# A Fourier mixing and maxout kernel on one core: the opening's loads, casts and table work put in another order

## The chip, the cores and the metric

The kernel runs on one NeuronCore of one Trainium2 chip. The metric is the time of one execution on the device in microseconds (us), median of several runs. The engines are TensorE (PE in the profile, its weight loads PEld), VectorE (DVE), ScalarE (ACT), GpSimd (POOL) and SyncE (SP), which here only issues DMAs. DMAs are issued by GpSimd (queue q0, which may also convert fp32 to bf16) and by SyncE (queue q1).

## The reference

Each of 8 batches of 3072 x 256 numbers is multiplied by a filter in the frequency domain, and the result goes through two matrices, a maximum and a third matrix:

```
X = np.fft.rfft(x, axis=1)
Y = X * (filt_r + 1j * filt_i)[None]
y = np.fft.irfft(Y, n=3072, axis=1)          # 8 x 3072 x 256
h1 = y @ w1;  h2 = y @ w2                    # 256 -> 1024
out = np.maximum(h1, h2) @ w_out             # 1024 -> 256
```

## The kernel before

The transform is split as 3072 = 96 x 32. The first stage multiplies by a 96-point table C1, the second (s2, L379) by a table U; a product with the filter F follows (product, L388), then the inverse stages with tables VP and VQ, and a last 96-point table G1 (s4, L454) that gives y for a tile of 384 rows. The second part uses max(h1, h2) @ w_out = relu(y (w1 - w2)) @ w_out + y (w2 @ w_out): Wd = w1 - w2 is made by GpSimd in four parts (prep_wd, L296), M = w2 @ w_out by TensorE (prep_t and prep_m, from the cast w2b and Wo). moe_h (L476) makes one of eight 128-wide parts of relu(y Wd) for a tile (ph, gt), moe_o (L519) the output sums (po).

All is written in a fixed order by hand (manual_schedule): each engine executes its instructions in program order, and waits only where data or a buffer needs it. PSUM tiles come from two pools: ps with six banks, pso with two.

Batch 0 has a path of its own. Its x comes in eight chunks of 4 x 256 columns on 96 partitions (load_x, L84; issued by GpSimd, converted to bf16); the filter F comes in sixteen DMAs (load_f, L111), also by GpSimd, into half of the partitions, and is doubled into the other half by VectorE for the first eight column groups (double_f, L128) and by SyncE's DMAs for the last four (L130). Rows with index 0 and 1536 come apart, in fp32 (FZ), and are put in by put_fz (L142, GpSimd) and fix_f (L145, VectorE). Then: s1t (L554) for the eight chunks, evicted by ScalarE (two of them by VectorE); transposes t1 (L566), evicted by VectorE and ScalarE in turn; s2 for six visits v; table_v and put_v, which make VP and VQ from U; products (L657), of which VectorE makes most and GpSimd those of v = 0, 2, 3, 4 for one half (from a copy xs that ScalarE makes) and a quarter of v = 5; s3t (L577) for v = 1, 0, 2, 3, 4, 5, each with a matmul on ones (W1) ahead that fills its wait, evicted into zT; transposes t2 (L599) and s4(0). U is made in two halves by ScalarE's sine (sines_u, L247). spin (L615) is a matmul whose result nobody reads.

x of batch 1 comes in four loads of two chunks (L680, L694, L698), and Wo by load_wo (L293), all by GpSimd between its products and prep_wd, then cast_w2. f1 (L323) is the first stage of batch 1: a matmul per pair of columns (pa), a copy to at, and after each second one a DMA to a DRAM tensor ad; f1_read (L340) reads it back in another order into bt, in three DMAs (u0 to u1).

From L777 on the main loop runs over 64 tiles and eight steps j each. At each step it emits moe_h, the listed visits (mid), part of moe_o of the tile before, and the planned small works (todo). Steps of batch 0 are numbered 0 to 63; plan(b, step, ...) puts a work at a step. plan_f2 (L733) places for the batch after next the loads of x to XF (load_xf, by SyncE, three buffers) and the folds (fold, GpSimd), and the visits of the batch that is next. ph is L482, po L534 and L536, and GpSimd issues the output DMAs (L495).

Of the kernel before, what the change touches and what calls it, by code (L numbers as in the profile page):

```python
# [8 lines left out]
FP32 = mybir.dt.float32  # L9
# [6 lines left out]
D = 256  # L16
HID = 1024
NP = 96
# [9 lines left out]
def kernel(  # L28
# [105 lines left out]
    def load_fn():  # L134
        for ri, f in enumerate((filt_r, filt_i)):
            for q in range(2):
                src = bass.AP(f.tensor, f.offset + 48 * q * D, [[96 * D, 16], [1, D]])
                nc.sync.dma_start(out=FZ[16 * q:16 * q + 16, ri], in_=src)
        nc.sync.dma_start(out=FZ[32:33, 0], in_=filt_r[1536:1537, :])
# [2 lines left out]
        G.tensor_copy(F[0:32, ri, 0, 0], FZ[0:32, ri])  # L142

    def fix_f():
        V.tensor_copy(F[32:33, 0, 0, 0], FZ[32:33, 0])  # L145


    V.memset(W1, 1.0)
# [5 lines left out]
    jb = init.tile([128, 16], FP32)  # L154
    cid = init.tile([128, 128], FP32)

    hv = init.tile([128, 2, 1], FP32)
    load_x(0, 0, 1)
    G.iota(pid, pattern=[[1, 1]], base=0, channel_multiplier=1, allow_small_or_imprecise_dtypes=True)
    G.iota(kc, pattern=[[2, NW], [24, 2], [1, 2]], base=0, channel_multiplier=0,  # L160
           allow_small_or_imprecise_dtypes=True)
    load_x(0, 1, 1)
    G.iota(kap, pattern=[[2, NW], [24, 2]], base=0, channel_multiplier=0,
           allow_small_or_imprecise_dtypes=True)
    G.iota(jb, pattern=[[1, 16]], base=0, channel_multiplier=0, allow_small_or_imprecise_dtypes=True)
    load_x(0, 2, 1)
    G.iota(cid, pattern=[[1, 128]], base=0, channel_multiplier=0, allow_small_or_imprecise_dtypes=True)
    for c in range(3, 8):
        load_x(0, c, 1)
    for q in range(2):  # L170
        G.memset(hv[:, q], 1.0)
        for r in (0, 32):
            G.memset(hv[r:r + 1, q], 0.5 * (1 - q))
    load_fn()
    for ri in range(2):
        put_fz(ri)
    load_f(0)
    load_f(1)

    def table_c():  # L180
        p96 = init.tile([128, 1], FP32)
        V.tensor_scalar(p96, pid, 1.0 / 96.0, None, OP.mult)
        uc = init.tile([NP, 48, 2], FP32)
        rc = init.tile([NP, 48, 2], FP32)
        kf = kc.rearrange("p w g s -> p (w g s)")
        V.tensor_scalar(uc[:, :, 0], kf, p96[0:NP], 0.25, OP.mult, OP.add)
        V.tensor_scalar(uc[:, :, 1], kf, p96[0:NP], None, OP.mult)
        V.tensor_scalar(uc[:, 0:1, 1], pid[0:NP], 0.5, 0.25, OP.mult, OP.add)
        V.tensor_scalar(rc, uc, RND, RND, OP.add, OP.subtract)
        V.tensor_tensor(uc, uc, rc, OP.subtract)  # L190
        S.activation(C1, uc.rearrange("p k r -> p (k r)"), AF.Sin, bias=zero[0:NP], scale=TWO_PI)

    def table_ct():
        G.memset(CT, 0.0)
# [52 lines left out]
    def sines_u(h):  # L247
        uv = ua.rearrange("p u c s j -> p u (c s j)")
        S.activation(U[:, NW * h:NW * h + NW], uv[:, NW * h:NW * h + NW], AF.Sin, bias=zero, scale=TWO_PI)

    def table_g():
        pg = ps.tile([96, NP], FP32, tag="ps", name="pg")
        TE.matmul(pg, C1, I128[0:NP, 0:NP], start=True, stop=True)
        S.activation(G1, pg, AF.Copy)

    def table_v(h, q):
# [16 lines left out]
    def put_v(h, q, pv):  # L273
        for s in range(2):
            i0 = 1 if h == 0 and s == 0 else 0
            tab = VQ if q else VP
            if i0:
                S.activation(tab[:, 0, 0], pv[0][:, 0], AF.Identity, bias=zero, scale=hv[:, q])
            S.activation(tab[:, 6 * h + i0:6 * h + 6, s], pv[s][:, i0:6], AF.Copy)  # L279
# [40 lines left out]
    zd = {}  # L320
    at_ = {}

    def f1(b, c, engine):  # L323
        if c == 0:
            ad[b] = dram.tile([96, NM, D], BF16, tag="ad", name="ad")
        if c % 4 == 0:
            at_[b] = apool.tile([128, 8, D], BF16, tag="at", name="at")
        at = at_[b]
        pa = ps.tile([96, 2, D], FP32, tag="ps", name="pa")
        TE.matmul(pa, C1, xb[b, c // 2][:, 2 * (c % 2):2 * (c % 2) + 2], start=True, stop=True)  # L330
        o_ = at[0:96, 2 * (c % 4):2 * (c % 4) + 2]
        if engine is V:
            V.tensor_copy(o_, pa)
        else:
            S.activation(o_, pa, AF.Copy)
        if c % 2 == 1:
            m0 = 2 * (c % 4) - 2
            nc.sync.dma_start(out=ad[b][:, 2 * c - 2:2 * c + 2], in_=at[0:96, m0:m0 + 4])

    def f1_read(b):  # L340
        bt[b] = bpool.tile([128, NU, D], BF16, tag="bt", name="bt")
        src = ad[b].rearrange("(u q) m d -> (q m) u d", q=4)
        for u0, u1 in ((0, 4), (4, 12), (12, NU)):
            nc.sync.dma_start(out=bt[b][:, u0:u1], in_=src[:, u0:u1])


    def s1(b, c):
# [227 lines left out]
            V.tensor_copy(bt[0][:, 4 * n:4 * n + 4], pb)  # L575

    def s3t(v, pq):  # L577
        pool, tag = (ps, "ps") if v % 2 else (pso, "po")
        pz = [pool.tile([128, 2, 2, 2, 2, NM], FP32, tag=tag, name="pt%d" % g) for g in range(2)]
        for _ in range(2 if v == 1 else 1):  # L580
            TE.matmul(pz[0].rearrange("p i s r c m -> p (i s r c m)"), W1[:, 0:128], W1, start=True, stop=True)  # L581
        for i in range(2):
            for s in range(2):
                for dc in range(2):
                    for q, tab in enumerate((VP, VQ)):
                        for g in range(2):
                            TE.matmul(pz[g][:, i, s, :, dc], pq[s][64 * g:64 * g + 64, q, i, 128 * dc:128 * dc + 128],  # L587
                                      tab[64 * g:64 * g + 64, 2 * v + i, s].rearrange("p (r m) -> p r m", r=2),
                                      start=(q == 0), stop=(q == 1))
        zv = zT.rearrange("p c m (w g) q -> p w g (c m) q", g=2)  # L590
        for g in range(2):
            o_ = zv[:, 2 * v:2 * v + 2, g]
            i_ = pz[g].rearrange("p i s r c m -> p i (c m) (s r)")
            if v >= 4 and g == 1:
                V.tensor_copy(o_, i_)
            else:
                S.activation(o_, i_, AF.Copy)

    def t2(c, engines):  # L599
        if c == 0:  # L600
            zr[0] = zrpool.tile([96, NM, D], BF16, tag="zr", name="zr")
        n = 4 // len(engines)
        for k, engine in enumerate(engines):
            pr = ps.tile([96, n, D], BF16, tag="ps", name="pr")
            m0 = 4 * c + n * k
            for m in range(n):
                for dc in range(2):
                    TE.transpose(pr[:, m, 128 * dc:128 * dc + 128], zT[:, dc, m0 + m].rearrange("p u q -> p (u q)"),  # L608
                                 I128)
            if engine is V:  # L610
                V.tensor_copy(zr[0][:, m0:m0 + n], pr)
            else:
                S.activation(zr[0][:, m0:m0 + n], pr, AF.Copy)
# [23 lines left out]
        if c < 7:  # L637
            spin(2)
    bt[0] = bpool.tile([128, NU, D], BF16, tag="bt", name="bt")
    zT = bpool.tile([128, 2, NM, NU, 4], BF16, tag="bt", name="zT")  # L640
    for n in range(6):
        t1(n, S if n % 2 else V)
    put_v(0, 0, table_v(0, 0))
    for g in range(2):
        for ri in range(2):
            double_f(0, g, ri, V)
# [22 lines left out]
    put_v(0, 1, table_v(0, 1))  # L669
    pxs[2] = s2(0, 2)  # L670
    stage_x(2)
    sines_u(1)
    put_v(1, 0, table_v(1, 0))
    pxs[3] = s2(0, 3)
    stage_x(3)
# [1 line left out]
    for v in (1, 0, 2):  # L677
        pqs[v] = products(v)
        if v == 0:
            load_x(1, 0, 2)  # L680
    s3t(1, pqs[1])
    pxs[4] = s2(0, 4)
    stage_x(4)
# [7 lines left out]
        pqs[v] = products(v)  # L691
    for v in (4, 5):
        s3t(v, pqs[v])
    load_x(1, 2, 2)  # L694
    load_wo()
    prep_wd(0, G)
    for c in (4, 6):
        load_x(1, c, 2)  # L698
    for q in range(1, 4):
        prep_wd(q, G)  # L700
    for h in range(2):
        cast_w2(h)
    table_ct()
# [4 lines left out]
    ypool = ctx.enter_context(tc.tile_pool(name="ypool", bufs=7))  # L708
    cepool = ctx.enter_context(tc.tile_pool(name="cepool", bufs=3))
    gpool = ctx.enter_context(tc.tile_pool(name="gpool", bufs=2))  # L710
    f1(1, 0, S)
    spin(1)
    t2(0, (V, S))
    f1(1, 1, V)
    spin(1)
    s4(0)
    f1(1, 2, S)
    f1(1, 3, V)


    todo = {}
# [4 lines left out]
    def plan_f1(b, nb, steps, read):  # L726
        for c, n in zip(range(4, 16), steps):
            plan(b, n, f1, nb, c, S if c % 2 == 0 else V)
        plan(b, read, f1_read, nb)

    mid = {}

# [15 lines left out]
            plan(b, steps[-1] + (6 if b else 11), s1_read, b + 2)  # L748

    plan(0, 1, t2, 1, (V,))  # L750
    plan(0, 7, prep_t, 0)
    plan(0, 9, prep_m)
    for c, n in ((2, 7), (4, 22), (5, 32), (6, 40), (7, 48)):
        plan(0, n, t2, c, (V,))
    plan_f1(0, 1, (5, 6, 7, 7, 9, 9, 10, 10, 11, 11, 12, 12), 13)
    plan_f2(0, (25, 28, 31, 35, 38, 42, 46), ((0,), (), (1,), (2,), (3,), (4,), (5, 6)),
            (8, 8, 10, 12, 17, 20, 24, 28), (10, 13, 16, 20, 24, 27, 30, 33))
    for b in range(1, B - 1):
        first = b == 1
        plan_f2(b, (15 if first else 14, 19 if first else 18, 23, 31, 34 if b < B - 2 else 35, 39, 47),  # L760
# [68 lines left out]
```

## Time and profile before

| | |
|---|---|
| median of the runs | 497.7 us (496.92 to 498.1, 3 runs) |
| the profiled execution's own time | 498.64 us |
| its span, first to last instruction | 496.8 us |
| TensorE busy | 483.8 us, 97% of the span, 5759 matmuls |
| VectorE, ScalarE, GpSimd busy | 335.4, 320.4, 258.7 us |
| mean granted clock of TensorE | 0.989 |
| first chunk of x taken by TensorE | 5.19 us |
| last chunk of x taken by TensorE | 14.21 us |
| first ph of the main loop | 37.73 us |
| first po | 44.19 us |

The profile is of one execution; the difference between its own time and its span lies around the first and the last instruction. A row of the timeline gives the start, the time until the last of its instructions ends, the engine, the line, the operation with its tiles, how many, and in brackets how long the engine had been idle and what ended that. Weight loads may run ahead of matmuls; matmul ends are modelled. "to landing" is the time from the start of a DMA's issue to the arrival of its data.

### The profile page before, as it was taken

The page shows a single profiled execution, that of the slowest core. Times are in us where ns is not written, and L with a number is a line of the kernel's source. Part 1 is how long each engine was busy: PE and PEld are TensorE (multiplying, and loading weights), DVE is VectorE, ACT ScalarE, POOL GpSimd, SP SyncE. Part 2 cuts the span into 40 slices and gives each one's busy share as a digit, 9 for nine tenths or more (in the row PEclk, how much of TensorE's full clock was granted, in tenths as well). Part 3 has the DMA queues.
Part 4 walks back from the last instruction along what each step waited for, and adds up shares of the span by engine and source line. Part 5 has one row for each costly group of instructions (what it writes and reads, how often), then busy time and mean ns, then how long its engine had stood idle before and what let it go on. Part 6 is the DMA issues. An engine that isn't in the chain of part 4 may idle for free.

```text
span 496.8 us, 14137 instructions
## 1 busy us (share of the span) xinstructions
PE 483.8 (97%) x5759; PEld 353.5 (71%) x5759; DVE 335.4 (68%) x535; ACT 320.4 (64%) x667; POOL 258.7 (52%) x342
## 2 busy tenths in 40 slices
PE   7699999999999999999999999999999999999997
PEld 3457777777777777777777777776777777777775
DVE  7886788468855688467855688457873688556542
ACT  5777478667775677576866668665766656464442
POOL 8694868318466594528646295536842212222220
PEclk9879999999999999999999999999999999999999
DMA  8989988996789867896789977897776834531112
GB/s 128 161 242 224 259 269 260 284 234 190 204 266 221 216 210 223 249 225 174 231 257 227 183 244 211 257 215 168 227 231 175 181 104 129 157 120 66 64 64 86
DMA packets 76626, 97.30 MB, mean 196 GB/s; under 512 B 7985, under 2 KB 54354, under 8 KB 75186
## 3 DMA queue, kind: packets, MB, share of 16 engines
q1 hardware_dynamic: 63218, 66.71, 52.1%
q0 software_dynamic: 13200, 29.60, 21.4%
q8 instruction: 45, 0.74, 0.7%
q14 instruction: 19, 0.16, 0.1%
q10 hardware_dynamic: 144, 0.09, 0.1%
HBM read 53.87 MB, written 47.19 MB: 203 GB/s over the span
## 4 chain that ended last, share of the span: by engine, by line
PE 92%; DMA 3%; ACT 2%; POOL 1%; issue 1%; DVE 0%; SPq 0%; POOLq 0%
PE po L536 34%; PE ph L482 33%; PE po L534 8%; PE pz L408 5%; PE pc L443 3%; PE px L384 2%; PE pa L355 2%; DMA xb<-in_x_dram 2%; DMA zr<-zd 1%; PE pt L587 1%; DMA zd<-zt 1%; PE pr L608 1%; POOL xb L89 1%; PE pt L581 1%; PE pa L330 1%
## 5 line engine op out<-in xcount | busy, mean ns | idle before, releaser
L486 ACT ACTIVATE gt<-ph 128x384 bf16<-128x384 f32 x357 | 175.7, 496 | 138.8 <-PE ph L482 136.2
L536 PE MATMUL po<-Wo,gt 128*128 128x256 bf16 x1528 | 262.7, 273 | 1.2 <-issue 1.2
L536 PEld LDWEIGHTS <-gt 128*128 128x128 bf16 x1528 | 144.7, 98 | 68.1 <-issue 13.5
L495 POOL DMA_DIRECT2D out_dram<-ot x186 | 103.1, 558 | 154.7 <-DVE ot L547 138.7
L390 DVE TENSOR_TENSOR pq<-px,F 128x1024 bf16<-128x1024 f32 x91 | 106.9, 1218 | 25.7 <-PE px L384 25.4
L484 DVE TENSOR_SCALAR gt<-ph 128x384 bf16<-128x384 f32 x155 | 83.6, 551 | 53.5 <-PE ph L482 47.1
L482 PEld LDWEIGHTS <-Wd 128*128 128x128 bf16 x1024 | 99.6, 98 | 13.7 <-issue 0.3
L104 POOL TENSOR_TENSOR xb<-XF 128x512 bf16<-128x512 f32 x48 | 61.3, 1277 | 66.9 <-DMA XF<-in_x_dram 31.7
L547 DVE TENSOR_SCALAR ot<-po 128x512 f32<-128x512 f32 x83 | 57.0, 686 | 35.0 <-PE po L536 33.1
L105 POOL TENSOR_TENSOR xb<-XF 128x512 bf16<-128x512 f32 x48 | 61.1, 1274 | 0.0
L359 ACT ACTIVATE at<-pa 128x512 bf16<-128x512 f32 x96 | 51.8, 611 | 3.4 <-PE pa L355 3.3
L412 ACT ACTIVATE zt<-pz 128x512 bf16<-128x512 f32 x84 | 45.6, 594 | 5.7 <-PE pz L408 1.9
L448 ACT ACTIVATE ce<-pc 128x384 f32<-128x384 f32 x56 | 23.7, 490 | 6.7 <-PE pc L443 6.0
L408 PE MATMUL pz<-pq,VP 64*64 64x256 bf16 x336 | 22.2, 281 | 0.0
L384 PE MATMUL px<-bt,U 64*64 64x256 bf16 x384 | 20.4, 283 | 1.2 <-ACT VQ L279 0.7
L408 PE MATMUL pz<-pq,VQ 64*64 64x256 bf16 x336 | 21.1, 269 | 0.0
L408 PEld LDWEIGHTS <-VP 64*64 64x64 bf16 x336 | 10.0, 105 | 13.3 <-issue 12.7
L355 PE MATMUL pa<-xb,CT 64*64 64x512 bf16 x192 | 18.0, 377 | 0.0
L443 PEld LDWEIGHTS <-zr 48*128 48x128 bf16 x896 | 13.1, 93 | 4.8 <-issue 4.4
L443 PE MATMUL pc<-G,zr 48*128 48x48 bf16 x896 | 15.4, 180 | 0.3 <-DMA zr<-zd 0.3
L384 PEld LDWEIGHTS <-U 64*64 64x64 bf16 x384 | 10.6, 109 | 3.9 <-issue 3.6
L618 PE MATMUL pd<-W 128*128 128x512 bf16 x28 | 9.2, 437 | 1.5 <-DVE zero L150 1.5
(383 smaller groups left out, 632.1 us busy)
## 6 DMA issues: line engine op xcount, KB each, us to landing
out_dram<-ot POOLq DMA_DIRECT2D x186, 128.0 KB, 3.8
XF<-in_x_dram SPq DMA_DIRECT2D x96, 192.0 KB
ad<-at SPq DMA_DIRECT2D x56, 192.0 KB
zd<-zt SPq DMA_DIRECT2D x42, 256.0 KB
zr<-zd SPq DMA_DIRECT2D x56, 192.0 KB
bt<-ad SPq DMA_DIRECT2D x13, 768.0 KB
WS<-in_moe_w_dram SPq DMA_DIRECT2D x4, 512.0 KB
xb<-in_x_dram POOLq DMA_DIRECT2D x8, 192.0 KB, 5.6
```

The lines of the kernel that those rows point to most:

```text
L104: G.tensor_tensor(t_[:, 0], f[:, 0], f[:, 1], OP.add)
L105: G.tensor_tensor(t_[:, 1], f[:, 0], f[:, 1], OP.subtract)
L359: S.activation(at[:, m0:m0 + 2], pa[g], AF.Copy)
L390: E.tensor_tensor(pq, px.rearrange("p (o i) d -> p o i d", o=1).to_broadcast([128, 2, 2, D]), F[:, :, 2 * v:2 * v + 2, s], OP.mult)
L408: TE.matmul(pz[g][64 * s:64 * s + 64, i], tab[64 * g:64 * g + 64, 2 * v + i, s], pq[s][64 * g:64 * g + 64, q, i], start=(q == 0), stop=(q ...
L412: S.activation(zt[:, :, g], pz[g], AF.Copy)
L482: TE.matmul(ph, Wd[:, dc, 128 * j:128 * j + 128], y_[:, dc], start=(dc == 0), stop=(dc == 1))
L484: V.tensor_scalar(gt[tt][:, j], ph, 0.0, None, OP.max)
L486: S.activation(gt[tt][:, j], ph, AF.Relu)
L495: E.dma_start(out=dst, in_=ot[tt // 2][:, 3 * (tt % 2) + c])
L536: TE.matmul(p_, g_[:, n - 2, blk], Wo[:, n - 2], start=(e == 0), stop=(e == 9))
L547: V.tensor_scalar(ot[tt // 2][:, e - 1:e + 1], po[q // 2 % 2], SCALE, None, OP.mult)
```

## The change

Ten edits, nearly all in front of the main loop:

- x of batch 0: pairs of chunks for the first six, single loads for the last two
- load_f(0) ahead of put_fz; fix_f by GpSimd
- the first load of x of batch 1 ahead of GpSimd's first product, the second in the place of the first; the later two change places with prep_wd and load_wo
- the second sine of U ahead of the transposes t1
- s3t takes its PSUM tiles from ps for v = 0, 3, 5 and from pso for 1, 2, 4 (before: ps for odd v)
- zT is laid out with eight groups of four columns outermost, and the last visit (v = 5) is evicted in two parts, group 0 first; a second 96-point table CP has its columns in the order that this layout needs, and G1 is made from it
- f1 is split in f1_in (matmul) and f1_out (copy and DMA); the first four copies come later
- the filling matmuls around t2(0) and s4(0) write one pso tile, four rather than two
- f1_read is planned as three works at steps 13, 14 and 15
- loads and folds of x of batch 2 at later steps

```diff
 def fix_f():
-        V.tensor_copy(F[32:33, 0, 0, 0], FZ[32:33, 0])
+        G.tensor_copy(F[32:33, 0, 0, 0], FZ[32:33, 0])
...
-    load_x(0, 0, 1)
+    load_x(0, 0, 2)
...
-    load_x(0, 1, 1)
+    load_x(0, 2, 2)
...
-    load_x(0, 2, 1)
     G.iota(cid, pattern=[[1, 128]], base=0, channel_multiplier=0, allow_small_or_imprecise_dtypes=True)
-    for c in range(3, 8):
+    load_x(0, 4, 2)
+    for c in range(6, 8):
         load_x(0, c, 1)
...
     load_fn()
+    load_f(0)
     for ri in range(2):
         put_fz(ri)
-    load_f(0)
     load_f(1)
...
         S.activation(C1, uc.rearrange("p k r -> p (k r)"), AF.Sin, bias=zero[0:NP], scale=TWO_PI)
+        S.activation(CP.rearrange("p (g w c) -> p g w c", g=2, c=4),
+                     uc.rearrange("p (w g s) r -> p g w (s r)", g=2, s=2), AF.Sin, bias=zero[0:NP], scale=TWO_PI)
...
-        TE.matmul(pg, C1, I128[0:NP, 0:NP], start=True, stop=True)
+        TE.matmul(pg, CP, I128[0:NP, 0:NP], start=True, stop=True)
...
     def f1(b, c, engine):
+        f1_in(b, c)
+        f1_out(b, c, engine)
+
+    def f1_in(b, c):
+        pas[c] = ps.tile([96, 2, D], FP32, tag="ps", name="pa")
+        TE.matmul(pas[c], C1, xb[b, c // 2][:, 2 * (c % 2):2 * (c % 2) + 2], start=True, stop=True)
...
-    def f1_read(b):
-        bt[b] = bpool.tile([128, NU, D], BF16, tag="bt", name="bt")
+    def f1_read(b, u0, u1):
+        if u0 == 0:
+            bt[b] = bpool.tile([128, NU, D], BF16, tag="bt", name="bt")
         src = ad[b].rearrange("(u q) m d -> (q m) u d", q=4)
-        for u0, u1 in ((0, 4), (4, 12), (12, NU)):
-            nc.sync.dma_start(out=bt[b][:, u0:u1], in_=src[:, u0:u1])
+        nc.sync.dma_start(out=bt[b][:, u0:u1], in_=src[:, u0:u1])
...
-        pool, tag = (ps, "ps") if v % 2 else (pso, "po")
-        pz = [pool.tile([128, 2, 2, 2, 2, NM], FP32, tag=tag, name="pt%d" % g) for g in range(2)]
+        pool, tag = (ps, "ps") if v in (0, 3, 5) else (pso, "po")
+        pz = [pool.tile([128, 8, 2, 2, 2, 2, 4], FP32, tag=tag, name="pt%d" % g) for g in range(2)]
...
+        for o0, o1 in ((0, 1), (1, 8)) if v == 5 else ((0, 8),):
+            for g in range(2):
+                o_ = zT[:, o0:o1, :, :, g, 2 * v:2 * v + 2].rearrange("p o c m w q -> p o (c m) (w q)")
+                i_ = pz[g][:, o0:o1].rearrange("p o i s r c m -> p o (c m) (i s r)")
+                if v >= 4 and g == 1:
+                    V.tensor_copy(o_, i_)
+                else:
+                    S.activation(o_, i_, AF.Copy)
...
+    sines_u(1)
     for n in range(6):
         t1(n, S if n % 2 else V)
     put_v(0, 0, table_v(0, 0))
+    load_x(1, 0, 2)
...
-    sines_u(1)
     put_v(1, 0, table_v(1, 0))
...
         if v == 0:
-            load_x(1, 0, 2)
+            load_x(1, 2, 2)
...
-    load_x(1, 2, 2)
+    for q in range(2):
+        prep_wd(q, G)
+    load_x(1, 4, 2)
+    prep_wd(2, G)
     load_wo()
-    prep_wd(0, G)
-    for c in (4, 6):
-        load_x(1, c, 2)
-    for q in range(1, 4):
-        prep_wd(q, G)
+    load_x(1, 6, 2)
+    prep_wd(3, G)
...
-    f1(1, 0, S)
-    spin(1)
+    pd = pso.tile([128, 512], FP32, tag="po", name="pd")
...
+    f1_in(1, 0)
+    fill(1)
     t2(0, (V, S))
-    f1(1, 1, V)
-    spin(1)
+    f1_in(1, 1)
+    f1_in(1, 2)
+    fill(1)
     s4(0)
-    f1(1, 2, S)
-    f1(1, 3, V)
+    f1_in(1, 3)
+    f1_out(1, 0, S)
+    f1_out(1, 1, V)
+    fill(2)
...
-        plan(b, read, f1_read, nb)
+        for k, (u0, u1) in enumerate(((0, 4), (4, 12), (12, NU))):
+            plan(b, read + k, f1_read, nb, u0, u1)
...
     plan(0, 1, t2, 1, (V,))
+    plan(0, 1, f1_out, 1, 2, S)
+    plan(0, 2, f1_out, 1, 3, V)
...
-            (8, 8, 10, 12, 17, 20, 24, 28), (10, 13, 16, 20, 24, 27, 30, 33))
+            (8, 8, 13, 14, 19, 26, 32, 38), (10, 13, 23, 27, 32, 34, 37, 42))
```

More of the change, by code (lines that the diff above doesn't have):

```diff
@@ L155 @@
     cid = init.tile([128, 128], FP32)
+    CP = init.tile([NP, 96], BF16)
     hv = init.tile([128, 2, 1], FP32)
-    load_x(0, 0, 1)
+    load_x(0, 0, 2)
     G.iota(pid, pattern=[[1, 1]], base=0, channel_multiplier=1, allow_small_or_imprecise_dtypes=True)
@@ L321, with f1_out @@
     at_ = {}
+    pas = {}
     def f1(b, c, engine):
+        f1_in(b, c)
[3 more added lines that the diff above has]
+        TE.matmul(pas[c], C1, xb[b, c // 2][:, 2 * (c % 2):2 * (c % 2) + 2], start=True, stop=True)
+    def f1_out(b, c, engine):
         if c == 0:
@@ L327, in f1 @@
             at_[b] = apool.tile([128, 8, D], BF16, tag="at", name="at")
-        at = at_[b]
-        pa = ps.tile([96, 2, D], FP32, tag="ps", name="pa")
-        TE.matmul(pa, C1, xb[b, c // 2][:, 2 * (c % 2):2 * (c % 2) + 2], start=True, stop=True)
+        at, pa = at_[b], pas.pop(c)
         o_ = at[0:96, 2 * (c % 4):2 * (c % 4) + 2]
@@ L577, in s3t @@
     def s3t(v, pq):
-        pool, tag = (ps, "ps") if v % 2 else (pso, "po")
-        pz = [pool.tile([128, 2, 2, 2, 2, NM], FP32, tag=tag, name="pt%d" % g) for g in range(2)]
+        pool, tag = (ps, "ps") if v in (0, 3, 5) else (pso, "po")
+        pz = [pool.tile([128, 8, 2, 2, 2, 2, 4], FP32, tag=tag, name="pt%d" % g) for g in range(2)]
         for _ in range(2 if v == 1 else 1):
-            TE.matmul(pz[0].rearrange("p i s r c m -> p (i s r c m)"), W1[:, 0:128], W1, start=True, stop=True)
+            TE.matmul(pz[0].rearrange("p o i s r c m -> p (o i s r c m)"), W1[:, 0:128], W1, start=True, stop=True)
         for i in range(2):
@@ L586, in s3t @@
                         for g in range(2):
-                            TE.matmul(pz[g][:, i, s, :, dc], pq[s][64 * g:64 * g + 64, q, i, 128 * dc:128 * dc + 128],
-                                      tab[64 * g:64 * g + 64, 2 * v + i, s].rearrange("p (r m) -> p r m", r=2),
+                            TE.matmul(pz[g][:, :, i, s, :, dc].rearrange("p o r m -> p r o m"),
+                                      pq[s][64 * g:64 * g + 64, q, i, 128 * dc:128 * dc + 128],
+                                      tab[64 * g:64 * g + 64, 2 * v + i, s].rearrange("p (r o m) -> p r o m", r=2, m=4),
                                       start=(q == 0), stop=(q == 1))
[L590 to L597, printed above, removed]
+        for o0, o1 in ((0, 1), (1, 8)) if v == 5 else ((0, 8),):
[6 more added lines that the diff above has]
+                    S.activation(o_, i_, AF.Copy)
     def t2(c, engines):
@@ L607, in t2 @@
                 for dc in range(2):
-                    TE.transpose(pr[:, m, 128 * dc:128 * dc + 128], zT[:, dc, m0 + m].rearrange("p u q -> p (u q)"),
+                    TE.transpose(pr[:, m, 128 * dc:128 * dc + 128],
+                                 zT[:, (m0 + m) // 4, dc, (m0 + m) % 4].rearrange("p g w q -> p (g w q)"),
                                  I128)
@@ L639 @@
     bt[0] = bpool.tile([128, NU, D], BF16, tag="bt", name="bt")
-    zT = bpool.tile([128, 2, NM, NU, 4], BF16, tag="bt", name="zT")
+    zT = bpool.tile([128, 8, 2, 4, 2, NW, 4], BF16, tag="bt", name="zT")
+    sines_u(1)
     for n in range(6):
@@ L710, with fill @@
     gpool = ctx.enter_context(tc.tile_pool(name="gpool", bufs=2))
-    f1(1, 0, S)
-    spin(1)
+    pd = pso.tile([128, 512], FP32, tag="po", name="pd")
+    def fill(n):
+        for _ in range(n):
+            TE.matmul(pd, W1[:, 0:128], W1, start=True, stop=True)
+    f1_in(1, 0)
+    fill(1)
     t2(0, (V, S))
-    f1(1, 1, V)
-    spin(1)
+    f1_in(1, 1)
+    f1_in(1, 2)
+    fill(1)
     s4(0)
-    f1(1, 2, S)
-    f1(1, 3, V)
+    f1_in(1, 3)
+    f1_out(1, 0, S)
+    f1_out(1, 1, V)
+    fill(2)
     todo = {}
```

## The prediction, put down before the changed kernel ran

> **What bounds the kernel now.** I read the page first: its slices, then the chain that ended last.
>
> ```profile
> PE   7699999999999999999999999999999999999997
> ...
> PEclk9879999999999999999999999999999999999999
> ...
> PE 92%; DMA 3%; ACT 2%; POOL 1%; issue 1%; DVE 0%; SPq 0%; POOLq 0%
> ```
>
> TensorE is full from the fourth slice on (12.4 us each). Time can be won in front of that point, or lost by a hole behind it. The edits all act in the first 90 us. In the second view, two-microsecond windows, the columns are busy time of TensorE, its weight loads, VectorE, ScalarE and GpSimd, then granted clock, DMA share and GB/s.
>
> ```profile
> 18.00:20.00 2.00, 1.28 (x46) 0.79 (x44) 1.97 (x3) 2.00 (x5) 1.67 (x3) 1.00 1.08 153
> ...
> 22.00:24.00 2.00, 0.46 (x11) 0.06 (x8) 1.78 (x4) 1.52 (x3) 0.80 (x2) 0.50 0.63 127
> 24.00:26.00 2.00, 1.70 (x81) 1.14 (x82) 2.00 (x2) 1.36 (x3) 2.00 (x2) 0.50 0.60 152
> ...
> 30.00:32.00 2.00, 1.89 (x44) 0.97 (x42) 1.97 (x3) 1.57 (x3) 2.00 (x2) 0.62 1.05 315
> ...
> 40.00:42.00 2.00, 2.00 (x24) 1.41 (x22) 1.91 (x5) 1.87 (x5) 2.00 (x3) 1.00 1.19 200
> ```
>
> TensorE waits most at 18 to 24 us, and then runs at half clock; VectorE and GpSimd are full there. From 36 on TensorE has no holes, but GpSimd stays full to 42. So I took the timeline of GpSimd third:
>
> ```profile
> 18.11 0.49 POOL L122 DMA_DIRECT2D F<-in_filt_r_dram  x1 [0.34 <-DMA F<-in_filt_r_dram]
> 18.82 1.01 POOL L122 DMA_DIRECT2D F<-in_filt_r_dram  x1 [0.22 <-issue]
> 19.82 2.40 POOL L122 DMA_DIRECT2D F<-in_filt_i_dram  x2
> 23.43 2.12 POOL L390 TENSOR_TENSOR pq<-xs,F 128x1024 bf16<-128x1024 f32 x1 [1.20 <-DVE F L128]
> ...
> 33.51 0.93 POOL L294 DMA_DIRECT2D Wo<-in_moe_w_out_dram  x1
> ...
> 36.72 3.74 POOL L298 TENSOR_TENSOR Wd<-WS 128x512 bf16<-128x512 f32 x3
> 40.40 2.01 POOL L291 CAST w2b<-WS 128x1024 bf16<-128x1024 f32 x2
> ```
>
> From its first product (23.43) GpSimd works without a pause to its last cast (42.41). TensorE's timeline shows how close it follows: the weight load of Wd columns 768 on stands at 40.55, and GpSimd finishes them at 40.46; the transposes of w2b stand at 41.48, its first cast ends at about 41.42. TensorE does not wait visibly, yet it could not have come much sooner.
>
> **The change part by part**
>
> *x in pairs.* Five loads in place of eight. At present TensorE takes chunks 0 to 7 at 5.19, 7.17, 8.23, 9.20, 10.93, 11.85, 12.85 and 14.21. A pair is usable only when both chunks are in, which by itself is a loss: behind chunk 5, ScalarE still has six evictions of about 0.40 and the sine of U (0.94). If pair 3 came at 11.85, as chunk 5 does, ScalarE would end at 11.85 + 0.38 + 3.3 = 15.6, against 15.08 now: 0.5 later. But the DMA listing gives 16-engine time per data packet: 2 KB packets (x of batch 0) take 204 to 251 ns at 4.5 to 10 us; 4 KB packets (x of batch 1, 25.8 to 31.8, with other traffic) take 330 ns. A pair is six packets for each of the 16 engines, a chunk six of half the size. The slowest engine now has the 36 packets of chunks 0 to 5 through from 3.0 (first packets) to 11.5, 236 ns each; an estimate for 18 packets of 4 KB, with that engine some 8% above the row, is 18 x 355 ns = 6.4 us, so pair 3 lands near 9.7, the range 9 to 11.9. With less than 10.3, ScalarE is never idle from the bias rows (6.08 now, 0.35 sooner because cid no longer stands behind a third load): 5.7 + 1.36 + 0.23 + 0.94 + 14 x 0.40 = 13.8, and VectorE, with its tables done at 13.15 and two copies of 0.55, ends at 14.25, against 15.32 now. I take **1.05 us** sooner; the ends are 0.5 late and 1.1 sooner.
>
> *Row fix to GpSimd.* VectorE loses 0.28 + 0.19 before its first product (23.76). GpSimd gets a one-row copy; nearest rows are its 32x256 casts (0.52 to 0.61) and 1x1 memsets (0.11). I take 0.5, in the 1.20 us that GpSimd now idles before 23.43.
>
> *x of batch 1 ahead of the products.* The first load (0.56) leaves its place at 25.50 and goes into the same idle time; the second load then takes that place, so the products do not move against each other. GpSimd has 3 issues fewer (1.6 us) in front. Each of its DMAs from the ninth on waits for the landing of the eighth before it, which the stalls at 12.09, 13.09 and 14.45 show; with x sooner these move too. I put the last F issue at 19.9 to 20.8 (now 22.22), the load at 1.0 to 1.2 (like the issues at 18.82 and 19.82, under VectorE's copies), the fix at 0.5: ready at 21.5 to 22.5. VectorE's copies, 18.49 to 23.25 now, end at 22.2. So product 0 starts at 22.4 to 22.5: **0.95 sooner**; ends: 0.3 later and 1.1 sooner.
>
> [...]
>
> *U's second sine earlier; PSUM pools alternate.* TensorE's 1.5 us wait for U (pv, L265) goes; the sine (0.93) fits in ScalarE's idle 1.34 before 16.43. v = 2 no longer needs the banks that v = 0 has just filled (ScalarE empties them until 31.17; its matmuls start at 31.25). What is late next: VectorE's products for v = 1, ready at 24.7; the table evictions, about 24.4; then GpSimd's last product, now 33.00, then 32.05. The last L587 group now starts at 34.05, a microsecond behind GpSimd; it would start at 32.3 and end at 33.0, against 34.73: 1.75 sooner. Half clock for 7 us (0.97 instead of 0.65 a group) is kept in this.
>
> *zT in parts.* The transposes wait for 64 elements rather than 512 a row: VectorE 0.69 becomes about 0.2 (bounds 0.1 and 0.4, by its 1x256 row at 0.28): 0.5 off, though the rest (0.6) stands in front of the zr copy and gives back 0.1. The at copies leave the way of y. Two more fill matmuls (0.22 each) lie beside those copies. First ph: 1.75 + 0.5 = **2.2 sooner**, 35.5. CP, one more 0.38 sine, lies in ScalarE's wait 4.3 to 6.08: nothing.
>
> *Wd sooner.* From the end of its products GpSimd now needs 7.40 to the w2b cast; then two Wd parts 2.46, a load 0.55, one part 1.23, Wo 0.93, a load 0.55, the last part 1.23 = 6.95. So 0.95 + 0.45 = **1.4 sooner** for the last Wd part (39.0) and the cast (40.0). TensorE would want them 2.2 sooner. It waits about 0.8 there: the gain is cut to 1.4.
>
> *Wo.* It is issued later: 32.05 + 4.24 = 36.3 instead of 33.51. It now lands 10.6 later, at 44.1, and the first po reads it at 44.19. Wanted by then: 44.19 - 1.4 = 42.8. It now sits behind a pair of x (landed 39.75) that shared with WS; after that it took 4.35. Then: issue ends 37.25, the pair before it is through by 38.1, 3.7 to 4.4 for 1024 packets at 58 to 68 ns, 0.4 to land: 42.2 to 42.9. Just in time; the bounds are 42.2 and 46.9 (10.6 again).
>
> *Exchange read in pieces; x of batch 2 later.* No px waits at 61.82, so no gain; the first piece is no longer queued on SP behind loads that wait for a fold. The fold of chunk 7 moves from step 33 to 42, with s1 at step 50 (89.5): about 80 + 2.5 us of GpSimd ends by 84. Nothing, 0 to 0.5 lost.
>
> **Sum.** 1.4 us off. The profiled execution took 498.64 in all, span 496.8; so 497.24, span 495.4. The median shown is 0.94 under that execution: 497.7 - 1.4 = **496.3**.
>
> **The rivals**
> 1. *Wo is late (slower).* Place: the first po of step 8. If Wo needs its present 10.6 us, it lands at 46.9, 2.7 behind the present 44.19: 500.4. It decides from a landing after 44.2 on, 7.9 us after issue. For: 512 B packets, TensorE has nothing else in order. Against: WS is through by then.
> 2. *Pairs land no sooner.* All behind moves 0.5 later, only the shorter GpSimd queue (0.45) and the row fix are left; gain 0 to 0.5: 497.4.
> [...]
> 4. *GpSimd does not bind*, since its queue shortens more than I count or TensorE's 2.2 mostly survives: 495.5.
>
> **How the numbers follow.** Forecast 0.43, rivals 0.10, 0.20, 0.15, 0.12. A difference under 0.2% (1.0 us) is about what cannot be told from none. Faster: 0.38 of the forecast, 0.12, 0.03 and 0.02 of rivals 4, 3 and 2 = 0.55. Slower: 0.10 of rival 1 and 0.04 of rival 2 (pairs 0.5 late and Wo late with them) = 0.14. Same: 0.31. The range 495.1 to 498.2 takes in cases 2 to 4 and leaves out most of rival 1 and a little below.
>
> **What would show it.** Chunk 4 taken by TensorE near 9.7 to 10.3; VectorE's first F copy at 17.4; GpSimd's first product at 22.4; the last L587 group (L598 there) at 32.3; the first ph at 35.5; then a visible wait of TensorE for GpSimd's Wd or w2b near 39 to 40, and none for Wo. Wrong: a wait of po for DMA Wo; first product after 23; chunk 4 after 11; a new hole between 45 and 100 us.

## The result, and the profile after

| | before | after |
|---|---|---|
| median of the runs | 497.9 us (496.92 to 498.76, 6 runs) | 501.82 us (500.53 to 503.37, 6 runs) |
| ratio to before | | 1.0083, 95% interval 1.0064 to 1.0101 |
| profiled execution: own time, span | 498.64, 496.8 us | 501.56, 499.8 us |
| first ph | 37.73 us | 39.50 us |
| first po | 44.19 us | 47.30 us |

The change costs 3.9 us, where 1.4 us of gain was forecast. First the page of the kernel after: TensorE's slices, its clock and the chain that ended last.

```profile
PE   6779999999999999999999999999999999999996
...
PEclk9969999999999999999999999999999999999999
...
PE 87%; DMA 7%; POOL 3%; issue 1%; SPq 0%; ACT 0%; POOLq 0%; DVE 0%; ACTq 0%
```

TensorE's first four slices read 6, 7, 7, 9 where they read 7, 6, 9, 9, and in the chain TensorE's share has fallen from 92% to 87% of the span, while that of DMAs has risen from 3% to 7% and GpSimd's from 1% to 3%. The two-microsecond windows of the kernel after (same columns as before) show where TensorE now stands.

```profile
18.00:20.00 2.00, 1.80 (x54) 1.49 (x52) 1.77 (x3) 2.00 (x3) 2.00 (x5) 1.00 0.93 123
22.00:24.00 2.00, 0.84 (x37) 0.64 (x39) 2.00 (x2) 1.85 (x5) 1.96 (x3) 0.88 0.78 180
24.00:26.00 2.00, 1.43 (x56) 0.81 (x52) 1.90 (x3) 1.92 (x5) 1.92 (x2) 0.50 0.83 140
...
46.00:48.00 2.00, 1.14 (x15) 0.91 (x12) 0.73 (x2) 1.29 (x2) 0.00 (x0) 1.00 1.02 198
```

In the opening TensorE waits in the same stretches, about a microsecond later, and the products pause behind 30 us for the doubled F rows (F<-F: VectorE 2.85 us, GpSimd 1.51 us), which they do not in the kernel before. 46 to 48 us has a hole; in the kernel before it was full:

```profile
46.00:48.00 2.00, 2.00 (x17) 1.53 (x16) 0.24 (x1) 0.67 (x2) 0.00 (x0) 1.00 0.90 265
```

GpSimd's timeline after:

```profile
22.02 1.26 POOL L89 DMA_DIRECT2D xb<-in_x_dram  x1
23.32 1.23 POOL L145 CAST F<-XF 1x256 bf16<-1x256 f32 x1
24.64 2.12 POOL L401 TENSOR_TENSOR pq<-xs,F 128x1024 bf16<-128x1024 f32 x1
...
33.01 2.13 POOL L401 TENSOR_TENSOR pq<-xs,F 128x1024 bf16<-128x1024 f32 x1 [1.51 <-DMA F<-F]
...
39.95 0.93 POOL L297 DMA_DIRECT2D Wo<-in_moe_w_out_dram  x1
...
42.62 2.02 POOL L294 CAST w2b<-WS 128x1024 bf16<-128x1024 f32 x2
```

The first product stands at 24.64 (23.43 before), Wo's issue at 39.95 (33.51 before). The wait view of TensorE from 44 us to 110 us, empty before, has two rows:

```profile
PE po L547 <- DMA Wo<-in_moe_w_out_dram: 0.9, 1, 0.9
PE pa L366 <- POOL xb L105: 0.5, 1, 0.5
```

The second row is a wait for a fold of x of batch 2, whose new steps the prediction had put at nothing, 0.5 us lost at most. To see which stretch loses how much, I took the start of the first ph of each of the 64 tiles (L482 before, L493 after) and subtracted before's. In the table, tile 1 lies ahead of Wo, "behind Wo" is tile 2 (53.56 us before), "ahead of the fold" tile 6 (87.03), "behind the fold" tile 7 (94.14). Positive is later than the kernel before. Each row comes from one profiled execution.

| kernel | first ph | tile 1 | behind Wo | ahead of the fold | behind the fold |
|---|---|---|---|---|---|
| after | +1.77 | +2.10 | +3.12 | +3.12 | +4.05 |
| wo_first | -0.38 | +0.85 | +0.86 | +0.86 | +1.35 |
| change_folds_old | -0.40 | +0.74 | +2.47 | +2.47 | +2.47 |
| wo_first_folds_old | +1.86 | +1.90 | +1.90 | +1.90 | +1.90 |
| c7_ahead | +0.29 | +0.33 | +0.34 | +0.34 | +0.34 |
| before_wo_late | -0.30 | +0.87 | +2.20 | +2.19 | +2.20 |
| before_folds_late | -0.57 | -0.35 | -0.34 | -0.27 | +3.70 |
| tables_and_zt | -1.45 | -0.76 | -0.76 | -0.76 | -0.76 |

The kernels are explained below. Three places lose: the opening up to the first ph (which varies most between executions), Wo, and a fold at 90 us. Where the first ph stands early, a fourth shows between it and tile 1 (1.1 to 1.2 us in wo_first, change_folds_old and before_wo_late). Later the differences shrink, and the last tile stands only 2.85 later in the kernel after: at 336 us the kernel before has in its own profile an idle stretch of 1.2 us that waits for no data ("issue"), the kernel after one of 0.6, and this accounts for half of the 1.2 us by which the difference shrinks.

### The profile page after: what moved, and what is told of

It reads as the page before. It is cut to its first block, busy times and chain, and to the rows that moved or that the text cites. A ratio compares the mean times of both kernels' runs of the same rounds, so it can differ in the third digit from the quotient of the medians.

```text
span 499.8 us, 14138 instructions
## 1 busy us (share of the span) xinstructions
PE 484.6 (97%) x5757; PEld 355.0 (71%) x5761; DVE 334.9 (67%) x535; ACT 321.0 (64%) x669; POOL 257.0 (51%) x340
## 4 chain that ended last, share of the span: by engine, by line
PE 87%; DMA 7%; POOL 3%; issue 1%; SPq 0%; ACT 0%; POOLq 0%; DVE 0%; ACTq 0%
PE po L547 34%; PE ph L493 32%; PE po L545 8%; PE pz L419 5%; PE pc L454 3%; PE pa L366 2%; PE px L395 2%; DMA xb<-in_x_dram 2%; DMA Wo<-in_moe_w_out_dram 1%; DMA F<-in_filt_i_dram 1%; DMA F<-F 1%; DMA XF<-in_x_dram 1%; POOL F L122 1%; POOL Wd L301 1%; POOL xb L89 0%
## 5 line engine op out<-in xcount | busy, mean ns | idle before, releaser
L493 PEld LDWEIGHTS <-Wd 128*128 128x128 bf16 x1024 | 99.5, 98 | 13.8 <-POOL Wd L301 0.4
```

Of the source, the lines that this page charges most:

```text
L493: TE.matmul(ph, Wd[:, dc, 128 * j:128 * j + 128], y_[:, dc], start=(dc == 0), stop=(dc == 1))
```

## The experiments

Theory A: Wo's load is too late (rival 1 of the prediction). Theory B: the opening's loads are what loses (pairs, and x of batch 1 ahead of the products). A third theory, C, came out of the table above after the first four runs: the new steps for x of batch 2. All medians stand beside the runs of the kernel before on the same chip; the first four, the next four and the last four rows come from three chips, on which the kernel before differs by 0.2 us at most.

| kernel | median us (runs) | before us (runs) | ratio, 95% interval |
|---|---|---|---|
| x1_old_place | 503.89 (4) | 497.82 (16) | 1.0118, 1.0081 to 1.0155 |
| x0_singles | 502.36 (5) | 497.82 (16) | 1.0070, 1.0034 to 1.0107 |
| singles_x1_old | 502.48 (6) | 497.82 (16) | 1.0088, 1.0059 to 1.0118 |
| wo_first | 500.06 (10) | 497.82 (16) | 1.0050, 1.0025 to 1.0075 |
| before_wo_late | 500.4 (10) | 497.66 (29) | 1.0050, 1.0034 to 1.0067 |
| before_folds_late | 502.9 (8) | 497.66 (29) | 1.0094, 1.0063 to 1.0125 |
| wo_first_folds_old | 498.1 (12) | 497.66 (29) | 1.0012, 0.9995 to 1.0029 |
| tables_and_zt | 497.35 (12) | 497.66 (29) | 0.9997, 0.9979 to 1.0014 |
| change_folds_old | 500.05 (6) | 497.81 (29) | 1.0053, 1.0034 to 1.0073 |
| c7_ahead | 498.62 (12) | 497.81 (29) | 1.0021, 1.0008 to 1.0034 |
| before_pairs | 497.86 (12) | 497.81 (29) | 1.0002, 0.9988 to 1.0016 |
| tables_fix_wd | 497.62 (12) | 497.81 (29) | 1.0004, 0.9990 to 1.0018 |

**The loads undone.** x1_old_place: the first two loads of x of batch 1 back in their old places (behind product 0, and ahead of the Wd parts), the rest as changed.

```diff
-    load_x(1, 0, 2)
...
-            load_x(1, 2, 2)
+            load_x(1, 0, 2)
...
+    load_x(1, 2, 2)
     for q in range(2):
         prep_wd(q, G)
```

> Only the loads of x of batch 1 go back: the first behind GpSimd's product 0, the second behind all its products. Theory 1 (these loads share the 16 DMA engines with the F<-F copies and so delay them: the last lands 5.8 us after its issue in the changed kernel, and product 3 waits 2.9 us for it): F<-F lands near 28.5, the wait of DVE pq for DMA F<-F is gone, GpSimd's last product ends 1.5 us sooner, and the time falls by 1 to 1.5 us against the changed kernel, to about 500.5; part is lost to Wo, which then stands behind one more pair. Rival (the pairs of batch 0 are the delay and all behind only follows): wait and time stay, 501.5 to 502.

x0_singles: x of batch 0 in eight loads as before, the rest as changed.

```diff
-    load_x(0, 0, 2)
+    load_x(0, 0, 1)
...
-    load_x(0, 4, 2)
-    for c in range(6, 8):
+    for c in range(3, 8):
         load_x(0, c, 1)
```

> Only the loads of x of batch 0 are eight singles again. Theory 2 (a pair is usable late and its 4 KB packets bring nothing): TensorE takes chunk 7 near 14.2 instead of 15.2, VectorE's first F copy starts near 18.5 instead of 19.5, everything behind is 1 us sooner: 500.8. If theory 1 alone counts, F<-F still lands near 32.6 and the time stays at 501.8.

singles_x1_old: both of these.

> Both load edits undone; the other eight stay (row fix on GpSimd, F ahead of the zero rows, sine of U, PSUM pools, zT in parts, Wd ahead of Wo, split first stage, exchange in pieces). If theories 1 and 2 hold and add: 2 to 2.5 us below the changed kernel, 499.5, with Wo the last wait of TensorE (landing 7 us or more after an issue near 38). If the eight others bring the 1.4 us that were forecast: 496.5.

wo_first: only Wo's load moved, ahead of the Wd parts.

```diff
+    load_wo()
     for q in range(2):
         prep_wd(q, G)
     load_x(1, 4, 2)
     prep_wd(2, G)
-    load_wo()
     load_x(1, 6, 2)
```

> Only load_wo goes back ahead of prep_wd. Theory 3 (the wait of the first po for Wo, 0.86 us in the profile, is all that Wo costs): the wait goes, Wd and w2b come 0.93 later and TensorE waits for them instead: within 0.5 us of 501.8. If TensorE is in truth held by Wo alone: 500.9.

Undoing the loads brought nothing: the three kernels stay at 502.4 to 503.9 us (x1_old_place highest, with a further wait of 1.4 us for the exchange read, bt from ad, that ends at 119.56 us). Their first ph stood at 37.35 to 37.65, as early as before, so the 39.50 of the profile after was a late execution of an opening that varies; and yet they lost at Wo, issued at 38.6 to 39.4, with waits of the first po of 2.3, 1.9 and 2.4 us. Theory B falls, and none of the three gains that were expected came. Moving Wo alone took 1.8 us off the median (0.9 was the most expected), with its issue at 33.39 and no wait for it. Theory A holds for that part, but 2.2 us over before remained. In the table of tiles wo_first loses twice: 1.2 us between the first ph and tile 1, where its ph waits 0.5 us for a Wd part, and 0.5 us at 87 to 94 us, where the three others lose 0.7 to 1.8. That second place is where TensorE comes to chunk 7 of batch 2.

**One part alone, and both undone.** before_wo_late is the kernel before with only the changed order of Wd parts, loads and Wo behind GpSimd's products.

```diff
     load_x(1, 2, 2)
+    for q in range(2):
+        prep_wd(q, G)
+    load_x(1, 4, 2)
+    prep_wd(2, G)
     load_wo()
-    prep_wd(0, G)
-    for c in (4, 6):
-        load_x(1, c, 2)
-    for q in range(1, 4):
-        prep_wd(q, G)
+    load_x(1, 6, 2)
+    prep_wd(3, G)
```

> The kernel before, with one thing of the change alone: GpSimd's issues and Wd parts behind its products in the changed order (two Wd parts, a pair of x, a third part, then Wo, a pair, the last part). Theory (Wo is issued too late, nothing else of the opening matters much): Wo is issued near 38.5 instead of 33.5, lands near 46 to 47.5, the first po stands at 46.5 to 47.5 instead of 44.2 with a wait for DMA Wo of 2 to 3 us; time 2.3 to 3.3 us over the kernel before. Rival (the opening as changed, its loads and its late parts, is what loses, and Wo only takes up slack that the opening has lost already): Wo lands before the first po wants it, no wait, time within 0.5 us of before.

Measured: 2.7 us over before. In its profile Wo is issued at 38.72 and lands 7.6 us later; GpSimd's first Wd part and TensorE's first po wait. From the wait views of GpSimd (20 to 45 us) and of TensorE (44 us on):

```profile
POOL Wd L298 <- DMA WS<-in_moe_w_dram: 0.9, 1, 0.9
```

```profile
PE po L536 <- DMA Wo<-in_moe_w_out_dram: 1.2, 1, 1.2
```

Both rows are absent in the kernel before. The Wd parts, moved ahead, run into the landing of WS, which Wo's issue had covered, and TensorE then waits for them (its wait view, 36 to 44 us):

```profile
PE ph L482 <- POOL Wd L298: 0.9, 1, 0.9
```

So the loss has two pieces in the table of tiles, 1.2 us between the first ph and tile 1 and 1.3 us at Wo; the wait of the first po is about half of the 2 to 3 us expected.

before_folds_late is the kernel before with only the new steps for x of batch 2.

```diff
-            (8, 8, 10, 12, 17, 20, 24, 28), (10, 13, 16, 20, 24, 27, 30, 33))
+            (8, 8, 13, 14, 19, 26, 32, 38), (10, 13, 23, 27, 32, 34, 37, 42))
```

> The kernel before, with one thing of the change alone: the steps at which x of batch 2 is loaded (8, 8, 13, 14, 19, 26, 32, 38) and folded (10, 13, 23, 27, 32, 34, 37, 42). Theory (the new steps put the load and the fold of chunk 7 behind those of batch 3's first chunk, and TensorE comes to it first): a wait of pa (second transform, batch 2) for the fold on GpSimd at 89 to 91 us, 0.5 to 1.3 us, time 0.5 to 1.3 over the kernel before. Rival (that wait comes only because everything ahead of it on SyncE's queue is late by Wo): no wait at 89 us, time within 0.4 us of before.

Measured: 5.2 us over before, four times the upper end of what was expected; the place is the one expected. The eight runs spread from 499.12 to 504.51 us, and the profiled one took 501.36. The wait view of TensorE (44 us on), its timeline there, and its windows of one microsecond:

```profile
PE pa L355 <- POOL xb L104: 1.2, 1, 1.2
PE pa L355 <- POOL xb L105: 0.8, 1, 0.8
```

```profile
90.47 0.37 PE L355 MATMUL pa<-xb,CT 64*64 64x512 bf16 x1 [1.25 <-POOL xb L104]
91.69 0.64 PE L355 MATMUL pa<-xb,CT 64*64 64x512 bf16 x3 [0.85 <-POOL xb L105]
```

```profile
90.00:91.00 1.00, 0.37 (x1) 0.10 (x1) 0.00 (x0) 0.00 (x0) 1.00 (x2) 1.00 1.07 257
91.00:92.00 1.00, 0.31 (x3) 0.13 (x2) 0.00 (x0) 0.00 (x0) 1.00 (x2) 0.67 1.15 284
92.00:93.00 1.00, 1.00 (x7) 0.56 (x5) 0.10 (x1) 0.64 (x2) 0.84 (x3) 0.50 1.10 355
...
94.00:95.00 1.00, 1.00 (x7) 0.63 (x5) 0.53 (x1) 0.00 (x0) 1.00 (x2) 0.62 0.73 279
```

TensorE waits 2.1 us in two pieces, and the granted clock falls to 0.5 from about 91.3 to 94.8. The tile stands 4.0 us further behind, 1.9 more than the wait; half of the 3.4 us at half clock, 1.7, is an estimate of what that cost. So the wait is charged nearly twice. None of the other profiles has a half clock there, so it is part of why the steps cost more here than in the changed kernel (5.2 and 1.8). Why chunk 7 is late is seen in SyncE's timeline. Before:

```profile
71.08 1.15 SPq L94 DMA_DIRECT2D XF<-in_x_dram  x2
...
73.87 1.84 SPq L94 DMA_DIRECT2D XF<-in_x_dram  x2
75.82 2.44 SPq L413 DMA_DIRECT2D zd<-zt  x2
78.86 0.81 SPq L362 DMA_DIRECT2D ad<-at  x2
```

The first of these rows loads chunk 7 (step 28), the second the first chunk of batch 3 (step 34); the stores behind it belong to steps 35 and 38. In before_folds_late:

```profile
73.21 6.92 SPq L94 DMA_DIRECT2D XF<-in_x_dram  x4
80.25 0.94 SPq L413 DMA_DIRECT2D zd<-zt  x2
81.70 1.80 SPq L362 DMA_DIRECT2D ad<-at  x2
83.55 1.28 SPq L94 DMA_DIRECT2D XF<-in_x_dram  x2
```

Here the four loads of the first row are chunk 6 and batch 3's first chunk (steps 32 and 34), and chunk 7 comes last, at step 38. There are three XF buffers, so batch 3's first load needs the buffer that chunk 5's fold gives back at 79.3; that fold too has been moved (step 27 to 34). It holds SyncE's queue, with the stores zd and ad behind it, and then chunk 7. The fold of chunk 7 starts at 89.16 as its data lands; before, it was done at 79.5.

Two things make chunk 7 late, its own later step and the held queue. The stores of step 38, right in front of it, end at 83.50 here and at 79.67 before, with tile 6 0.27 us earlier here. An estimate from these rows is that the held queue makes about 4 us of the 12.5 by which the load is issued later (83.55 against 71.08), the later step the rest. The same working gives 1 us for the held queue in wo_first and in the kernel after (the stores end at 81.59 and 83.76, with tile 6 0.86 and 3.12 us later than before).

That the queue is held longer here may be the exchange read: here it is one block of three DMAs, and one load of x waits 2.9 us on SyncE behind it. This was not tried by itself.

wo_first_folds_old is the changed kernel with Wo first and the old steps.

> The changed kernel with Wo issued ahead of the Wd parts and with the old steps for loading and folding x of batch 2. Theory (Wo and the fold of chunk 7 are the two losses of the change): no wait for Wo, none for the fold near 90 us, median 499 to 499.6, that is 0.5 to 1.0 under wo_first's 500.06; what remains above before (1.0 to 1.7) is GpSimd's Wd parts, about 1 us later because they wait for DMA WS. Rival (the fold steps cost nothing, another part of the change loses after 60 us): 500 again, and TensorE's ph groups stand further behind before's after 87 us than ahead of it.

Measured 498.1: the two losses together explain the result, 501.82 - 498.1 = 3.7 of the 3.9 us. That is 0.9 less than the lower end expected. (Its row in the table of tiles comes from an execution of 499.96 us with a late opening.) tables_and_zt keeps only the parts of the change that touch neither a load nor GpSimd: CP, U's sine, the PSUM pools, zT in parts, f1 split, fills, the read in pieces.

> The kernel before with only the parts of the change that touch neither a load nor GpSimd: the permuted sine (CP), U's sine earlier, PSUM pools alternating, zT in parts, first-transform copies apart, fill matmuls, exchange read in pieces; loads of x, F, Wo, Wd order, row fix and fold steps as before. Theory (these parts are worth the 0.1 to 0.4 us by which the first ph came sooner in the kernels with old loads, and no more): first ph at 37.3 to 37.7, first po at 43.8 to 44.2, time 0 to 0.4 us under before, which may not be told from none. Rival A (the prediction's step 3 holds when the loads are left alone): last s3t group a microsecond sooner, time 1 us under. Rival B (a part of these loses): first ph sooner but po or the steps behind 87 us later, time 0.5 or more over.

Measured 497.35, which cannot be told from before. Rival A falls, the theory's 0 to 0.4 holds.

**The two losses crossed, and the rest.** change_folds_old is the changed kernel with the old steps alone.

> The changed kernel with the old steps for loading and folding x of batch 2, all else as changed, Wo late too. Theory (two separate losses, Wo and the fold of chunk 7): the wait of the first po for Wo stays (1 to 2.5 us), no wait near 91 us; 1.8 to 2.7 us over wo_first_folds_old's 498.1, as Wo's place alone added 2.7 to the kernel before: 499.9 to 500.8, and 1 to 2 under the changed kernel's 501.8. Rival (the two hide one another: a late Wo delays the main loop and so gives the loads of chunk 7 time): about 501.8 as before the undoing.

Measured 500.05, 1.8 under the changed kernel; the wait for Wo is there, and it is the only row in its wait view of TensorE from 44 to 110 us, so none is left near 91:

```profile
PE po L547 <- DMA Wo<-in_moe_w_out_dram: 1.6, 1, 1.6
```

With wo_first (500.06) and wo_first_folds_old (498.1) this closes the square: each of the two undone alone is worth 1.8 us, the second on top of the first 1.9 to 2.0. These are differences of medians of 6 to 12 runs that spread over 3 to 5 us, so each is known to a microsecond or two; within that the two add up, and nothing shows that they hide one another.

c7_ahead is wo_first with chunk 7 alone put back ahead of batch 3's first chunk.

```diff
-            (8, 8, 13, 14, 19, 26, 32, 38), (10, 13, 23, 27, 32, 34, 37, 42))
+            (8, 8, 13, 14, 19, 26, 32, 33), (10, 13, 23, 27, 32, 34, 37, 39))
```

> As wo_first, but of the new steps only chunk 7's are put back: its load to step 33 and its fold to step 39, each just ahead of the first chunk of batch 3 (34 and 40). Theory (chunk 7 is late because SyncE holds its load behind batch 3's first load, which waits for the buffer that chunk 5's fold gives back): no wait for the fold near 91 us, median about 498.1 as with all old steps, at most 498.6. Rival (all loads are later, and the order of the last two is not what matters): a wait near 91 us of 0.5 or more stays, or a new one at chunk 3 to 6, median 499.5 to 500.

Measured 498.62 against 500.06: three quarters of what all old steps bring (498.1). In its profile SyncE issues the loads of chunk 6, chunk 7 and batch 3's first chunk together from 71.90, the fold of chunk 7 runs at 82.16, and TensorE does not wait near 91. So chunk 7's place on SyncE's queue is the mechanism. The edit moves its load five steps ahead as well as in front of batch 3's chunk, and its fold with it, so it does not part the held queue from the later step. For the 0.5 us that is left, which the medians hardly tell from none, its profile shows one wait that wo_first's lacks, at 99.47 us (the wait view of TensorE, 44 us on):

```profile
PE pc L454 <- DMA zr<-zd: 0.5, 1, 0.5
```

Tile 8, behind it, stands 0.6 us further behind than tile 7. Whether this wait comes in every execution is open.

before_pairs is the kernel before with only x of batch 0 in pairs.

> The kernel before with only the loads of x of batch 0 changed, the first six chunks in pairs. The prediction's step 1 says chunk 4 near 10 us, chunk 7 and all behind it a microsecond sooner: 496.6. Theory now (pairs land no sooner, as their packets are twice as long and the slowest engine counts): chunk 2 is taken near 9.5 to 10.5 instead of 8.2, chunk 7 at 14.2 to 15.2, the time 0 to 1.0 over before.

Measured 497.86 against 497.81: nothing. Chunk 2 is taken at 9.35 instead of 8.24, chunk 4 at 11.23 instead of 10.94, chunk 7 at 14.07 instead of 14.21.

tables_fix_wd was to be the version that beats both: tables_and_zt with the row fix on GpSimd, and the later loads of x spread behind the Wd parts.

```diff
-        V.tensor_copy(F[32:33, 0, 0, 0], FZ[32:33, 0])
+        G.tensor_copy(F[32:33, 0, 0, 0], FZ[32:33, 0])
...
     load_wo()
-    prep_wd(0, G)
-    for c in (4, 6):
-        load_x(1, c, 2)
-    for q in range(1, 4):
-        prep_wd(q, G)
+    for q in range(2):
+        prep_wd(q, G)
+    load_x(1, 4, 2)
+    prep_wd(2, G)
+    load_x(1, 6, 2)
+    prep_wd(3, G)
```

> A candidate that should be no slower than either: tables_and_zt with the row fix on GpSimd and, behind Wo, the Wd parts ahead of the later loads of x (two parts, pair, part, pair, part). Theory: VectorE's first product 0.3 to 0.45 sooner behind its copies, the last Wd part 0.3 to 0.5 sooner, no wait for x of batch 1: 0.2 to 0.6 under tables_and_zt's 497.35, that is 496.8 to 497.1, 0.1 to 0.2 per cent under before. [...]

Measured 497.62, where 496.8 to 497.1 was expected: it gains nothing that can be told, and why is not shown. No version tried beats the kernel before by more than the measurement can tell.

## Why the prediction was wrong, point by point

Two terms decide the miss: Wo, put as just in time (point 6), and the later steps of batch 2, put at nothing (point 7). The gains of points 1, 2, 3 and 5 did not come either.

1. *Pairs, 1.05 us sooner: wrong.* They land no sooner, as rival 2 said. The DMA listing of the first 16 us, before and then after (loads, KB each, median us to landing):

```profile
xb<-in_x_dram POOLq DMA_DIRECT2D x8, 192.0 KB, 5.6
```

```profile
xb<-in_x_dram POOLq DMA_DIRECT2D x3, 384.0 KB, 7.8
xb<-in_x_dram POOLq DMA_DIRECT2D x2, 192.0 KB, 10.0
```

The 4 KB packets take what I had estimated: 353 ns at 6 to 8 us in the kernel after, 355 estimated. But the saving a byte was too large: over 3 to 10 us they take 347 ns on average and the 2 KB packets of the kernel before 199, which is 13% less a byte where the sum had 25% (355 against 2 x 236), and at 6 to 8 us the 2 KB packets take 179, under the 204 to 251 of the prediction. Chunk 4, expected near 10 us, was taken at 12.47 and in before_pairs at 11.23. Chunks 2 and 3 now land together, the two single loads are issued 1.5 us sooner and so run among the pairs, and in the kernel after the first F load is issued at 6.00 instead of 8.66; which of these holds up the pairs is not shown. t1 started at 14.99 to 17.12 in seven profiles with pairs and at 14.49 to 15.81 in seven with single loads.

2. *GpSimd's first product 0.95 sooner: wrong.* It waits for the F copies and the tables, which come no sooner when t1 does not. From the start of t1 to the first product it was 8.29 us before and 8.53 after. Under VectorE's copies the load took 1.26 us (1.0 to 1.2 put) and the fix 1.23 (0.5 put), and the first product started 0.34 us behind the last copy, which ends at 24.30. VectorE did gain the fix: its first product starts 0.10 us behind its copies, 0.51 before. One reading was wrong too: at 22 to 24 us GpSimd is not full, it is busy for 0.80 of 2 us.

No run shows what the chances count as rival 3 (0.15). What the runs show is that the load and the fix took longer under VectorE's copies: behind them the next load of x of batch 1 took 0.56 us (at 26.70) and, in x0_singles, the fix 0.39, and here each took about as long as one copy (1.23 us). The load, issued at 22.02, was through at 23.28, a microsecond ahead of the last copy's end.

3. *U's sine and the PSUM pools, last s3t group 1.75 sooner: wrong.* TensorE's wait for U has gone, but the span from t1 to the last s3t group is 18.49 us in tables_and_zt against 18.91 before, and 18.51 and 18.53 in before_wo_late and before_folds_late, which lack these edits (the kernel before has a half clock of 10.2 us in its opening, the three others one of 6.8). In tables_and_zt as before, VectorE and GpSimd make their products without a pause, and these end last: GpSimd's last ends 17.86 us behind t1 before, 17.88 in tables_and_zt.

4. *zT in parts, 0.5: nearly right.* From the last s3t group to the first ph it was 3.68 us before, 3.69 in before_wo_late and before_folds_late, and 3.30 or 3.31 in most profiles with the new zT (3.53 in the profile after): 0.38. The split of f1 and the fills are in this too; none was tried alone.

5. *Wd 1.4 sooner: wrong.* The parts were moved to a place where WS has not landed, a wait that the sum does not have: it starts the first part at 32.05, and GpSimd waits 0.9 to 1.1 us for WS in before_wo_late, change_folds_old and wo_first, where that part starts at 34.4 to 35.4. The w2b cast, behind the last Wd part, starts at 41.3 to 41.4 there and at 42.62 in the profile after, instead of 40.40.

6. *Wo just in time: wrong, the step that decides half of the loss.* The working had its issue at 36.3 and 5.9 to 6.6 us to landing. The issue is 2.3 us later even in good openings (38.60 in change_folds_old: products 1.2 later than put, WS 1.1), 3.7 later in the profile after, and the landing took 7.3 to 8.9 us in the six kernels that issue it late. It lands at 46.3 to 47.9 in these, wanted at 44.2. My own rival 1 gave 10%; its point of decision, a landing after 44.2, was passed by 2 to 4 us. With the predicted issue and these landing times it would have come at 43.6 to 45.2, on both sides of that point and behind the 42.8 at which the prediction itself wanted it, so this rival deserved more than 10%.

7. *The steps of batch 2, "nothing, 0 to 0.5 lost": wrong, the other half.* I counted GpSimd's work (ended by 84 us) and not SyncE's queue. The load of chunk 7 had been put ten steps later, behind the stores of that step and behind a load that waits for a buffer. It cost 1.8 us.

All four signs named in the prediction as wrong came true: a wait of po for DMA Wo, the first product after 23 (24.64), chunk 4 after 11 (12.47) and a new hole between 45 and 100 us.

## What to carry to other kernels

When a load is moved later, follow it on the queue that issues it: what stands in front of it there, which buffer that one waits for, and whose work gives the buffer back; the work of the engine that uses the data says nothing of it. Work moved ahead gains only if its inputs land sooner too: here the Wd parts ran into WS, and pushed behind them a load that had been just in time. An edit that shows "just in time" by an estimate of a landing time should be given the spread of the landings that the traces show (7.3 to 10.6 us for Wo here), not one value.

## What was not expected of the hardware

- A wait of 2.1 us in two pieces, at 89 to 92 us of before_folds_late, went with about 3.4 us at half clock; the clock fell at 91.34, when TensorE had been idle for 1.75 us since 89.22. A wait of 2.3 us in one piece at 46 to 48 us of x1_old_place left the clock at 1.00. In the openings the half clock lasted 6.8 us (before_wo_late, before_folds_late) or 10.2 us (before, after), two or three times 3.4. What sets the clock is not shown: the length of a wait alone does not tell in these runs whether it falls.
- The same opening varies: with identical code up to the Wd parts, chunk 7 of x was taken at 14.19 us (wo_first) and at 16.20 (wo_first_folds_old), and a wait for the doubled F rows (F<-F) of 2 to 3 us came in the profile after (2.85) and in before_pairs (2.10), but not in wo_first, c7_ahead or change_folds_old.
